# Unsplit first-layer factors, a PReLU of two operations, and products summed in a bank that is read between them

## The chip, the cores and the metric

The kernel runs on one core of one Trainium2 chip. The metric is the device time of one execution in microseconds (us). Five engines work side by side: PE (TensorE, matmuls), DVE (VectorE), ACT (ScalarE), POOL (GpSimd) and SP (SyncE, which issues the transfers). They wait for each other by semaphores. Matmuls write into eight accumulation banks (PSUM); the other engines read these.

## The reference, cut to what matters

```
attn = softmax(mask(q @ k.T / 8)) @ v          # 4 batches, 8 heads, 576 positions, 64 each
x = attn as [2304, 512]                        # 2304 tokens
h = max(x @ w1, x @ w2, x @ w3)                # first network, 512 -> 768
x = h @ moe_w_out                              # 768 -> 512
h = x @ w_in                                   # second network, 512 -> 2048
g = max(h, 0) + alpha * min(h, 0)              # PReLU, one slope for each hidden column
return g @ moe2_w_out                          # 2048 -> 512
```

## The kernel before, in words

Every matmul works on a number split in two: a high part, rounded to the short form that TensorE multiplies fast, and a low part, the rest. A product is the sum of three matmuls (high by high, high by low, low by high; `PAIRS`). A split costs a cast for the high part, mostly on ACT, and a subtraction for the low part, mostly on DVE.

**Stage 1** (0 to about 318 us) is laid out by a planner, `Weave`, from costs, positions and rings of buffers given with `add(...)`. It runs the attention and the first network for batches 0 to 2 and turns the weights, which come as 64-bit floats, into 32-bit words: `from_double` loads them, `rebase` (ACT) and `join_words` (DVE) make a word. `pair_tasks` (L506) forms the factors of the second network: 16 calls, eight for w_in and eight for w_out. For w_in each call makes four factors, splits them (`store_tasks`) and stores high and low part to DRAM tiles `wh` (list `hd`).

**Stage 2** (about 318 to 388 us) is `last_net` (L684): the first network of batch 3. After 12 ordinary gate units it goes through six groups k = 3 to 8 of seven Strassen-like products each. A product is six matmuls of 288 columns into a bank of its own; DVE adds each bank to sums that lie in SBUF (u, v, w), takes the greatest of three gates (`greatest`) and, after the third, splits it (`make_lows`). Beside this ACT and POOL prepare inputs x2 of the second network for the next block (`early_sums`, `early_split`): POOL makes four sums, ACT casts the high part, POOL subtracts the low part, SP stores both (`xd`). At the end come eight output products.

**Stage 3** (about 388 to 748 us) is the second network: 3 blocks of 768 tokens, each with 8 units n (24 in all). `h_products(n)` gives seven products of six matmuls with 384 columns into two banks `ph` in turn; `o_units(n-1)` gives 12 pieces of three matmuls with 256 columns into banks `po`. The loop at the end weaves the two by hand through `units_before`. The copy of the first product goes to ACT; DVE adds the others to sums in SBUF (L1191); `hidden` then makes the PReLU, in `slopes` (two ACT operations) and `join` (one on DVE), and `split_g` splits the result. `sums` forms what the next layer's Strassen form needs. `defer(s, step)` puts a step off by s products. `load_h` fetches the factors for unit n+2 during unit n, high and low part, up to 512 KB each.

At a block's end (n = 7, 15, 23) the first pieces of `kept_units` use the two `ph` banks directly after the unit's products, the first bank in six matmuls (two pieces), the second in three; `prepare` splits kept sums for them, twice in product 5 of that unit.

## Time and profile before

| what | value |
|---|---|
| times of three runs | 749.99, 750.4, 751.33 us (median 750.4) |
| profiled execution | span 747.7 us; its time lies outside the profile, the median of the runs is 2.7 us above the span |
| PE busy | 732.9 us (98%), 5560 matmuls |
| DVE busy | 640.3 us (86%) |
| ACT busy | 464.5 us (62%) |
| POOL busy | 28.7 us (4%) |
| TensorE's granted clock | 1.00 of full speed in every slice |

The span is the time from the first to the last instruction on the engines. "Busy" is the time in which an engine executes something; an average over the span says nothing of one stage, so the rows further down are taken by stage. The ends of matmuls are modelled: consecutive matmuls overlap in the records.

### The profile page before, as it was taken

How to read it: one execution, taken by the hardware profiler on the slowest of the kernel's cores; microseconds unless marked ns; L12 is line 12 of the kernel's file. 1: busy time of each engine (PE TensorE's matmuls, PEld its weight loads, DVE VectorE, ACT ScalarE, POOL GpSimd, SP SyncE). 2: the span in 40 equal slices, each digit the busy share in tenths (PEclk: the TensorE clock that was granted, in tenths of full speed). 3: DMA queues.
4: the chain of work that ended last, by engine and by line, in shares of the span. 5: the costliest groups of instructions: out<-in, count | busy, mean ns of one | idle time of the engine just before them, and what ended most of it. 6: DMA issues, size and time to landing. Idle time of an engine off the chain costs nothing.

```text
span 747.7 us, 16003 instructions
## 1 busy us (share of the span) xinstructions
PE 732.9 (98%) x5560; PEld 710.3 (95%) x5560; DVE 640.3 (86%) x1711; ACT 464.5 (62%) x1254; POOL 28.7 (4%) x42
## 2 busy tenths in 40 slices
PE   5899999999999999999999999999999999999998
PEld 4699999999999999999999999999999999999997
DVE  4899999899898999478868898888989888988896
ACT  5987889568684788423345666634666654556571
POOL 1000000000000000023500000000000000000000
PEclk9999999999999999999999999999999999999999
DMA  7477769996999765779899789999789999867362
GB/s 248 155 244 227 234 206 337 342 342 244 323 318 340 252 219 208 253 267 332 306 319 400 266 293 332 383 401 372 265 286 316 364 401 369 289 236 254 118 201 77
DMA packets 88929, 211.96 MB, mean 283 GB/s; under 512 B 11024, under 2 KB 41232, under 8 KB 88848
## 3 DMA queue, kind: packets, MB, share of 16 engines
q1 hardware_dynamic: 88848, 210.94, 80.4%
q8 instruction: 44, 0.72, 0.4%
q14 instruction: 37, 0.30, 0.1%
HBM read 154.80 MB, written 56.10 MB: 282 GB/s over the span
## 4 chain that ended last, share of the span: by engine, by line
PE 94%; ACT 2%; DMA 2%; DVE 1%; issue 0%; SPq 0%; ACTq 0%; DVEq 0%
PE bank L580 24%; PE ph L1185 23%; PE po L986 15%; PE bank L602 10%; PE bank L753 4%; PE po L992 4%; PE ph L986 3%; PE bank L317 3%; PE bank L392 2%; PE bank L367 2%; PE po L996 2%; ACT e L332 1%; DMA wh<-w 1%; DMA k<-in_kTs 0%; PE po L1185 0%; DMA wo<-w 0%
## 5 line engine op out<-in xcount | busy, mean ns | idle before, releaser
L1185 PE MATMUL ph<-x,w 128*128 128x384 f32 x990 | 200.1, 337 | 0.0
L580 PE MATMUL bank<-x,w 128*128 128x288 f32 x1440 | 197.5, 296 | 0.0
L580 PEld LDWEIGHTS bank<-x,w 128*128 128x128 f32 x1440 | 191.8, 188 | 2.1
L1185 PEld LDWEIGHTS ph<-x,w 128*128 128x128 f32 x990 | 166.3, 188 | 1.0
L986 PE MATMUL po<-w,g 128*128 128x256 f32 x936 | 135.6, 281 | 0.0
L986 PEld LDWEIGHTS po<-w,g 128*128 128x128 f32 x936 | 130.1, 189 | 0.4
L1191 DVE TENSOR_TENSOR c<-ph,c 128x384 f32<-128x384 f32 x165 | 89.5, 555 | 30.5 <-PE ph L1185 27.4
L979 ACT CAST g<-c 128x384 fp32r<-128x384 f32 x93 | 47.0, 505 | 91.1 <-DVE c L1169 51.7
L602 PE MATMUL bank<-h,w 128*128 128x288 f32 x576 | 79.4, 297 | 0.0
L602 PEld LDWEIGHTS bank<-h,w 128*128 128x128 f32 x576 | 76.9, 188 | 0.9
L256 ACT CAST w<-word 128x512 fp32r<-128x512 f32 x100 | 58.0, 590 | 24.8 <-DMA wh<-w 7.9
L332 ACT ACTIVATE e<-e,nm 96x128 f32<-96x128 f32 (+2 forms) x176 | 68.1, 396 | 6.1 <-DVE nm L325 5.9
L259 DVE TENSOR_TENSOR w<-word,w 128x512 fp32r<-128x512 f32 x100 | 63.4, 642 | 9.2 <-ACT w L256 8.9
L1129 ACT ACTIVATE c<-c 128x384 f32<-128x384 f32 x96 | 50.5, 526 | 32.9 <-DVE c L1191 31.8
L1130 ACT ACTIVATE c<-c,nalpha 128x384 f32<-128x384 f32 x96 | 59.2, 617 | 3.1
L1134 DVE SCALAR_TENSOR_TENSOR c<-c 128x384 f32<-128x384 f32 x96 | 53.1, 553 | 6.1 <-ACT c L1130 6.1
L980 DVE TENSOR_TENSOR g<-c,g 128x384 fp32r<-128x384 f32 x96 | 53.0, 552 | 0.9 <-ACT g L979 0.5
L451 ACT ACTIVATE word<-raw 128x512 f32<-128x512 f32 x56 | 37.6, 682 | 14.6 <-DMA raw<-in_w 10.8
L980 DVE TENSOR_TENSOR g<-k,g 128x384 fp32r<-128x384 f32 x72 | 37.2, 558 | 7.5 <-ACT g L979 7.5
L992 PE MATMUL po<-w,g 128*128 128x512 f32 x120 | 43.0, 397 | 0.0
L457 DVE SCALAR_TENSOR_TENSOR word<-raw,word 128x512 uint32<-128x512 uint32 x56 | 38.8, 692 | 1.9
L1169 DVE TENSOR_TENSOR k<-c 128x384 f32<-128x384 f32 x72 | 37.9, 551 | 0.0
(107 smaller groups left out, 939.1 us busy)
## 6 DMA issues: line engine op xcount, KB each, us to landing
w<-wh SPq DMA_DIRECT2D x72, 512.0 KB, 5.3
raw<-in_w SPq DMA_DIRECT2D x50, 512.0 KB, 5.1
w<-wo SPq DMA_DIRECT2D x48, 512.0 KB, 5.8
w<-wp SPq DMA_DIRECT2D x36, 512.0 KB, 6.4
wh<-w SPq DMA_DIRECT2D x24, 512.0 KB, 5.0
xd<-xst SPq DMA_DIRECT2D x28, 384.0 KB, 3.2
x<-xd SPq DMA_DIRECT2D x28, 384.0 KB, 8.2
ws<-w SPq DMA_DIRECT2D x12, 512.0 KB, 5.4
```

Source lines behind the costliest of these rows:

```text
L256: (nc.scalar.copy if e == "ACT" else nc.vector.tensor_copy)(out_, in_)
L259: nc.vector.tensor_tensor(out=out_, in0=x, in1=y, op=ALU.subtract)
L332: nc.scalar.activation(tl[ek][:nq, j, i, :nk], tl[ek][:nq, j, i, :nk], AF.Exp, bias=tl["nm", u][:nq, j, i:i + 1], scale=-1.0, accum_out=tl ...
L580: nc.tensor.matmul(acc, words["gate", f, g][:, wi, cc * P:(cc + 1) * P], xt[b, cc, hf][:, xi, :], start=n == 0, stop=n == 3 * NCC - 1)
L602: nc.tensor.matmul(acc, words["mix", f][:, wi, dc * P:(dc + 1) * P], st["h", hf, f][:, xi, :], start=n == 0, stop=n == 3 * NF1 - 1)
L980: return g, lambda: nc.vector.tensor_tensor(out=g[:, 1], in0=x, in1=g[:, 0].bitcast(F32), op=ALU.subtract)
L986: nc.tensor.matmul(bank[:, NH * half:NH * (half + 1)], g[:, gi, t * P:(t + 1) * P], w[:, wi, off:off + NH], start=first and i == 0, stop=l ...
L992: nc.tensor.matmul(bank.rearrange("p (s n) -> p s n", n=NH), g[:, 0, t * P:(t + 1) * P], w[:, :, off:off + NH], start=first, stop=last)
L1130: nc.scalar.activation(a, a, AF.Copy, scale=nalpha[:, f:f + 1])
L1134: nc.vector.scalar_tensor_tensor(out=a, in0=h, scalar=0.0, in1=a, op0=ALU.max, op1=ALU.add)
L1185: nc.tensor.matmul(bank, words["h", n, i][:, wi, off + c * P:off + (c + 1) * P], x2h[blk, k, c][:, xi, :], start=m == 0, stop=m == 5)
L1191: nc.vector.tensor_tensor(out=out_, in0=bank, in1=other, op=ALU.add)
```

## The change

Three parts, in the words of the code:

- **Factors split at each fetch.** `wh` holds the factors of w_in as plain 32-bit words. `keep_task` stores them as they are in place of `store_tasks`, so the 32 splits of stage 1 fall away. `load_h` fetches half the bytes. After each fetch `high_h` (ACT, a cast) and `low_h` (DVE, a subtraction) split the factor: four of each for every unit n, 96 of each in all; those of units 0 and 1 stand in `last_net`, those of unit n+1 in unit n at its products 0, 1, 4, 5 and 6.
- **PReLU in two operations.** `g = max(h, alpha * h)` if the slope is at most 1. For a greater slope the sign of h, of alpha and of the second layer's factor is turned: `flip_sb` holds the sign bits, `join_words` puts them into the 16 words of w_out, `sign_sb` is 1 or -1. `hidden` is then one ACT operation (copy times sign) and one on DVE (times alpha, then the greater of the two). alpha is loaded at the start of the program instead of after stage 1.
- **Products that add up in a bank.** In both networks the products 11, T2, T3 and T4 go into one bank `grown`, with `start=False` after the first. Between two of them ACT copies what stands there (u, v, w). Products 21, T1 and 22 use the other bank or banks of their own; in stage 3 the last product adds to T1. DVE does three additions from banks in place of seven for each unit or group. The order of the products, `units_before` and the product at which `load_h` runs are changed. Unit 0 keeps four banks.

```diff
-    hd = [[dram.tile([P, 2, DM], F32, name=f"wh{q}_{i}") for i in range(4)] for q in range(NQ)]
+    hd = [[dram.tile([P, DM], F32, name=f"wh{q}_{i}") for i in range(4)] for q in range(NQ)]
...
+            nc.vector.tensor_scalar(out=a, in0=a, scalar1=3, scalar2=flip_sb[:, flip:flip + 1],
+                                    op0=ALU.logical_shift_left, op1=ALU.bitwise_xor)
...
+    def keep_task(key, ak, n, place, pos, given):
+        add(load(n // 2), lambda _: nc.sync.dma_start(place[:, :n], tl[ak][:, :n].bitcast(F32)), pos,
+            needs=[given], gives=[("stored", key)], uses=[ak])
...
+            def follow(left=0):
+                while len(lows) > left:
+                    h, t = lows.pop(0)
+                    nc.vector.tensor_tensor(out=h[:, 1], in0=t, in1=h[:, 0].bitcast(F32), op=ALU.subtract)
+                for hf, f, t in highs:
+                    h = st["h", hf, f] = hp.tile([P, 2, HALF], F32R, tag="x", name="h")
                     nc.scalar.copy(h[:, 0], t)
                     lows.append((h, t))
+                highs.clear()
+
+            u, v, w = (new() for _ in range(3))
+            grown = bank()[:, :HALF]
+            product(grown, w0, 0, "11")
+            nc.scalar.copy(u, grown)
+            follow()
+            yield
+            x = bank()[:, :HALF]
+            product(x, w0, 256, "21")
             add(u, x, u)
+            follow()
+            keep(0, 0, u)
+            yield
+            product(grown, sb, 256, "T2", False)
+            nc.scalar.copy(v, grown)
+            follow()
+            yield
+            y = bank()[:, :HALF]
+            product(y, sa, 0, "T1")
+            add(v, y, v)
+            follow()
+            yield
+            product(grown, sb, 0, "T3", False)
+            nc.scalar.copy(w, grown)
+            add(w, y, w)
+            follow()
+            keep(1, 1, w)
+            yield
+            x = bank()[:, :HALF]
+            product(x, sa, 256, "22")
             add(v, x, v)
...
+            product(grown, w1_, 256, "T4", False)
...
-                nc.sync.dma_start(t[:, :, :m].bitcast(F32), hd[n % NQ][i][:, :, :m])
+                nc.sync.dma_start(t[:, 1, :m].bitcast(F32), hd[n % NQ][i][:, :m])
+    def high_h(n, i):
+            nc.scalar.copy(t[:, 0, :m], t[:, 1, :m].bitcast(F32))
+    def low_h(n, i):
+            nc.vector.tensor_tensor(out=t[:, 1, :m], in0=t[:, 1, :m].bitcast(F32),
+                                    in1=t[:, 0, :m].bitcast(F32), op=ALU.subtract)
...
+    for m, i, n in ((0, 0, -12), (0, 2, -11), (0, 1, -5), (0, 3, -4), (1, 0, 3), (1, 2, 4), (1, 1, 5), (1, 3, 6)):
+        splits.setdefault(gates + n, []).append(lambda m=m, i=i: high_h(m, i))
+        splits.setdefault(gates + n + 1, []).append(lambda m=m, i=i: low_h(m, i))
...
-            nc.scalar.activation(a, h, AF.Relu, scale=-1.0)
-            nc.scalar.activation(a, a, AF.Copy, scale=nalpha[:, f:f + 1])
-            defer(1, join)
+            nc.scalar.activation(a, h, AF.Copy, scale=sign_sb[:, f:f + 1])
+            defer(soon, join)
...
-            nc.vector.scalar_tensor_tensor(out=a, in0=h, scalar=0.0, in1=a, op0=ALU.max, op1=ALU.add)
+            nc.vector.scalar_tensor_tensor(out=a, in0=h, scalar=alpha_sb[:, f:f + 1], in1=a,
+                                           op0=ALU.mult, op1=ALU.max)
...
+        product(2, grown, start=False)
+        nc.scalar.copy(v, grown)
         due()
         yield
+        product(3, other)
+        due()
+        yield
+        product(4, grown, start=False)
+        nc.scalar.copy(w, grown)
+        load_h(n + 2, (0, 2))
+        add(w, other, w)
+        hidden(n, 1, 1, w)
+        due()
+        yield
+        product(5, grown, start=False)
...
+        hidden(n, 1, 0, grown, 0)
...
+        product(6, other, start=False)
         load_h(n + 2, (1, 3))
+        add(v, other, v)
...
-        units_before = [i * 12 // 7 for i in range(8)]
+        units_before = [0, 1, 2, 3, 4, 8, 10, 12]
...
+                for half, m in {0: (("high", 0),), 1: (("low", 0),), 4: (("high", 2), ("low", 2), ("high", 1)),
+                                5: (("low", 1), ("high", 3)), 6: (("low", 3),)}.get(i, ()):
+                    (high_h if half == "high" else low_h)(n + 1, m)
```

How the change moves instructions is shown at three places. In the rows a name is a tile with its number, `<-` goes from what is written to what is read, and the waits name the engine or the transfer queue that the instruction waits for.

First ACT in stage 2, from the end of group 5 into group 6. `h` is a hidden tile's high part, `xst` an early split of x2, `t<-bank` a copy from a bank. Before:

```order
L766 CAST h_5557<-t_5364 128x288 [waits DVE_49]
L766 CAST h_5572<-t_5343 128x288 [waits DVE_49]
L211 CAST xst_5575<-xs_5459 128x384 [waits DMAHW6_49,DMAHW0_49,Pool_49]
L771 COPY t_5585<-bank_5578 128x288 [waits PE_49,Activation_49]
L211 CAST xst_5598<-t_5539 128x384 [waits DMAHW3_49,Pool_49]
L211 CAST xst_5619<-xs_5460 128x384 [waits DMAHW4_49,DMAHW0_49]
L211 CAST xst_5641<-t_5540 128x384 [waits DMAHW5_49]
L771 COPY t_5664<-bank_5657 128x288 [waits PE_49]
```

and in the changed kernel:

```order
L211 CAST xst_5458<-xs_5353 128x384 [waits DMAHW6_49,DMAHW0_49,Pool_49]
L786 COPY t_5461<-bank_5464 128x288 [waits PE_49,Activation_49]
L779 CAST h_5473<-t_5295 128x288 [waits DVE_49]
L211 CAST xst_5485<-xs_5354 128x384 [waits DMAHW3_49,DMAHW0_49,Pool_49]
L796 COPY t_5462<-bank_5464 128x288 [waits PE_49,Activation_49]
L211 CAST xst_5504<-t_5426 128x384 [waits DMAHW4_49,Pool_49]
L805 COPY t_5463<-bank_5464 128x288 [waits DVE_49,PE_49]
L211 CAST xst_5524<-xs_5353 128x384 [waits DMAHW5_49]
L821 COPY t_5537<-bank_5464 128x288 [waits DVE_49,PE_49]
```

One copy in a group has become three or four, each from the bank into which the next product of the group is added, and they stand between the casts of x2, which wait for POOL and for transfers.

Second PE in one unit of the second network (`ph` are the two banks, `po` the banks of the woven pieces). Before:

```order
L1185 MATMUL ph_7891<-x30_7175,w_7625 128x384 [waits DVE_49]
L1185 MATMUL ph_7891<-x30_7175,w_7625 128x384 x2
L1185 MATMUL ph_7891<-x31_7177,w_7625 128x384 x3
L986 MATMUL po_7798<-w_7511,g_7854 128x256 x3
L1185 MATMUL ph_7892<-x40_7197,w_7709 128x384 [waits DMAHW3_49,DVE_49]
L1185 MATMUL ph_7892<-x40_7197,w_7709 128x384 x2
L1185 MATMUL ph_7892<-x41_7199,w_7709 128x384 x3
L986 MATMUL po_7836<-w_7558,g_7878 128x256 [waits DMAHW1_49]
L986 MATMUL po_7836<-w_7558,g_7878 128x256 x5
L1185 MATMUL ph_7891<-x50_7226,w_7709 128x384 [waits DVE_49]
L1185 MATMUL ph_7891<-x50_7226,w_7709 128x384 x2
```

and in the changed kernel:

```order
L1240 MATMUL ph_7933<-x30_7060,w_7769 128x384 [waits DVE_49]
L1240 MATMUL ph_7933<-x30_7060,w_7769 128x384 x2
L1240 MATMUL ph_7933<-x31_7062,w_7769 128x384 x3
L1040 MATMUL po_7692<-w_7488,g_7894 128x256 x3
L1240 MATMUL ph_7932<-x40_7081,w_7716 128x384 [waits Activation_49]
L1240 MATMUL ph_7932<-x40_7081,w_7716 128x384 x2
L1240 MATMUL ph_7932<-x41_7083,w_7716 128x384 x3
L1040 MATMUL po_7724<-w_7488,g_7894 128x256 x6
L1040 MATMUL po_7733<-w_7533,g_7897 128x256 [waits DMAHW6_49]
L1040 MATMUL po_7733<-w_7533,g_7897 128x256 x5
L1240 MATMUL ph_7932<-x50_7122,w_7769 128x384 [waits Activation_49]
L1240 MATMUL ph_7932<-x50_7122,w_7769 128x384 x2
```

Before, products alternate between two banks and wait for DVE. Now four of them go into one bank (`ph_7932` here) and wait there for ACT, which copies it between them; a longer stretch of woven pieces stands ahead of the sixth product.

Third DVE around products 4 to 6 of a block's last unit. Here `g<-k` is the low part of a kept sum (`prepare`), `c<-ph` reads a bank, and `w<-w` the low part of a fetched factor. Before:

```order
L1191 TENSOR_TENSOR c_7190<-ph_7092,c_7169 128x384 [waits DVE_49,PE_49]
L1191 TENSOR_TENSOR c_7117<-ph_7092,c_7117 128x384
L980 TENSOR_TENSOR g_7173<-c_7144,g_7173 128x384 [waits Activation_49]
L980 TENSOR_TENSOR g_7213<-k_6236,g_7213 128x384 [waits Activation_49]
L980 TENSOR_TENSOR g_7216<-k_6384,g_7216 128x384 [waits Activation_49]
L1191 TENSOR_TENSOR c_7169<-ph_7091,c_7169 128x384 [waits DVE_49,PE_49]
L1134 SCALAR_TENSOR_TENSOR c_7192<-c_7190,c_7192 128x384
L1191 TENSOR_TENSOR c_7117<-ph_7092,c_7117 128x384 [waits DVE_49,PE_49]
```

and in the changed kernel:

```order
L1246 TENSOR_TENSOR c_6990<-ph_6987,c_6990 128x384 [waits Activation_49]
L909 TENSOR_TENSOR w_6917<-w_6917 128x512 [waits DMAHW5_49,Activation_49]
L1034 TENSOR_TENSOR g_7108<-k_6128,g_7108 128x384 [waits Activation_49]
L1034 TENSOR_TENSOR g_7111<-k_6277,g_7111 128x384 [waits Activation_49]
L1187 SCALAR_TENSOR_TENSOR c_7079<-c_6990,alpha_sb_65,c_7079 128x384 [waits DVE_49]
L1187 SCALAR_TENSOR_TENSOR c_7114<-ph_6986,alpha_sb_65,c_7114 128x384 [waits Activation_49]
L909 TENSOR_TENSOR w_6967<-w_6967 128x512 [waits DMAHW7_49]
L1246 TENSOR_TENSOR c_6989<-ph_6987,c_6989 128x384 [waits PE_49]
```

Both readings that free the `ph` banks for the first kept pieces (`c_7114<-ph_6986` and `c_6989<-ph_6987`) now stand behind the low parts of two kept sums and of fetched factors.

## Rows read from the trace of the kernel before

**Rows 1.** The page's head and its first part: busy time of each engine.

```profile
span 747.7 us, 16003 instructions
PE 732.9 (98%) x5560; PEld 710.3 (95%) x5560; DVE 640.3 (86%) x1711; ACT 464.5 (62%) x1254; POOL 28.7 (4%) x42
```

**Rows 2.** Windows: stretch, length, busy (count) of PE PEld DVE ACT POOL, PEclk, DMA share, GB/s.

```profile
0.00:40.00 40.00, 28.85 (x275) 22.69 (x276) 27.85 (x170) 32.48 (x140) 3.51 (x17) 1.00 0.63 204
40.00:740.00 700.00, 699.74 (x5253) 683.58 (x5252) 609.66 (x1536) 432.06 (x1115) 25.22 (x25) 1.00 0.83 290
```

**Rows 3.** Timeline of PE, 288-column matmuls of stages 1 and 2: start, us, what.

```profile
316.24 19.20 PE L580 MATMUL bank<-x,w 128*128 128x288 f32 x144
335.28 33.76 PE L753 MATMUL bank<-x,w 128*128 128x288 f32 x252
```

**Rows 4.** Timeline of PE and DVE: last product of one unit, first two of the next, its last.

```profile
440.00 1.22 PE L1185 MATMUL ph<-x,w 128*128 128x384 f32 x6
...
441.25 0.56 DVE L1191 TENSOR_TENSOR c<-ph,c 128x384 f32<-128x384 f32 x1 [0.74 <-PE ph L1185]
...
441.75 1.21 PE L1185 MATMUL ph<-x,w 128*128 128x384 f32 x6
...
443.15 1.22 PE L1185 MATMUL ph<-x,w 128*128 128x384 f32 x6
...
451.58 0.69 PE L1185 MATMUL ph<-x,w 128*128 128x384 f32 x3
```

**Rows 5.** ACT's groups by form: count | busy, mean ns of one | idle before, releaser.

```profile
L979 ACT CAST g<-c 128x384 fp32r<-128x384 f32 x93 | 47.0, 505 | 91.1 <-DVE c L1169 51.7 <-DVE c L1134 33.9 <-PE po L986 5.4
...
L256 ACT CAST w<-word 128x512 fp32r<-128x512 f32 x84 | 51.5, 624 | 17.6 <-DMA wp<-w 5.3 <-DMA wh<-w 5.0 <-DVE word L457 2.9
...
L1130 ACT ACTIVATE c<-c,nalpha 128x384 f32<-128x384 f32 x96 | 59.2, 617 | 3.1
...
L1195 ACT COPY c<-ph 128x384 f32<-128x384 f32 x24 | 11.3, 470 | 11.7 <-PE ph L1185 11.7
...
L771 ACT COPY t<-bank 128x288 f32<-128x288 f32 x6 | 2.4, 393 | 5.1 <-PE bank L753 5.1
```

**Rows 6.** DVE's groups by form.

```profile
L1191 DVE TENSOR_TENSOR c<-ph,c 128x384 f32<-128x384 f32 x165 | 89.5, 555 | 30.5 <-PE ph L1185 27.4 <-ACT c L1195 2.4
L259 DVE TENSOR_TENSOR w<-word,w 128x512 fp32r<-128x512 f32 x84 | 56.8, 685 | 6.3 <-ACT w L256 6.2
...
L733 DVE TENSOR_TENSOR t<-bank,t 128x288 f32<-128x288 f32 x42 | 18.4, 453 | 4.2 <-PE bank L753 1.5 <-ACT xst L211 1.1 <-ACT t L771 0.8
```

**Rows 7.** Timeline at the end of the first block (unit 7): the readings of the banks, and PE.

```profile
475.63 0.55 DVE L1191 TENSOR_TENSOR c<-ph,c 128x384 f32<-128x384 f32 x1
...
476.22 0.53 ACT L1129 ACTIVATE c<-c 128x384 f32<-128x384 f32 x1 [1.15 <-DVE c L1191]
...
476.50 1.77 PE L986 MATMUL ph<-w,g 128*128 128x256 f32 x13
476.56 0.56 DVE L1191 TENSOR_TENSOR c<-ph,c 128x384 f32<-128x384 f32 x1
```

**Rows 8.** Timeline of ACT in stage 2, the first group and group 6.

```profile
336.06 0.43 ACT L211 CAST h<-t 128x288 fp32r<-128x288 f32 x1 [0.75 <-DVE t L591]
336.40 0.76 ACT L211 CAST x<-t 128x288 fp32r<-128x288 f32 x2
337.07 0.39 ACT L771 COPY t<-bank 128x288 f32<-128x288 f32 x1
...
357.72 0.52 ACT L211 CAST xst<-t 128x384 fp32r<-128x384 f32 x1 [2.38 <-POOL t L831]
...
362.45 0.51 ACT L211 CAST xst<-xs 128x384 fp32r<-128x384 f32 x1 [3.10 <-DMA xd<-xst]
```

**Rows 9.** Timeline of POOL: the third sum of x2 in group 6, from which ACT casts.

```profile
356.57 1.11 POOL L831 TENSOR_TENSOR t<-xs 128x384 f32<-128x384 f32 x1
```

**Rows 10.** DMA issues: count, KB each, median us from issue to landing.

```profile
w<-wh SPq DMA_DIRECT2D x72, 512.0 KB, 5.3
```

More of the change, by code (lines that the diff above doesn't have):

```diff
@@ L445, in from_double @@
             uses=[rk])
-        add((("DVE", 1050),), lambda _: join_words(tl[rk], tl[ak]), pos, needs=[("up", key)],
+        add((("DVE", 1050),), lambda _: join_words(tl[rk], tl[ak], flip), pos,
+            needs=[("up", key)] + ([("slopes",)] if flip is not None else []),
             gives=[ak], uses=[rk, ak])
@@ L528, in pair_tasks @@
         if layer == 0:
-            store_tasks(("h", q, 0), ek, DM, [(0, hd[q][0][:, :, :])], pos, ek)
-            parts_ = ((1, ok, DM, [(0, hd[q][1][:, :, :])]), (2, sk[0], DM, [(0, hd[q][2][:, :, :])]),
-                      (3, sk[1], half, [(0, hd[q][3][:, :, :half])]))
+            keep_task(("h", q, 0), ek, DM, hd[q][0], pos, ek)
+            for i, k, n in ((1, ok, DM), (2, sk[0], DM), (3, sk[1], half)):
+                keep_task(("h", q, i), k, n, hd[q][i], late, ("sums", s))
+            return
         else:
@@ L746, in last_net, with product @@
             new = kept_temp if g == 0 else temp
-            def product(w, off, name):
-                bank_ = bank()[:, :HALF]
+            def product(bank_, w, off, name, start=True):
                 m = 0
@@ L753, in product, with keep @@
                         nc.tensor.matmul(bank_, w[:, wi, off + c * P:off + (c + 1) * P],
-                                         factors[name, c][:, xi, :], start=m == 0, stop=m == 5)
+                                         factors[name, c][:, xi, :], start=start and m == 0,
+                                         stop=m == 5, skip_group_check=True)
                         m += 1
-                return bank_
-            def greatest(hf, j, c):
+            def keep(hf, j, c):
                 if g == 0:
@@ L766, in greatest @@
                     nc.scalar.copy(h[:, 0], t)
                     lows.append((h, t))
-            x = product(w0, 0, "11")
-            u = new()
-            nc.scalar.copy(u, x)
-            yield
-            x = product(sb, 256, "T2")
-            v = new()
-            add(v, x, u)
-            make_lows()
+                highs.clear()
[3 more added lines that the diff above has]
+            nc.scalar.copy(u, grown)
@@ L793, in last_net @@
-            add(w, x, w)
+            x = bank()[:, :HALF]
+            product(x, sa, 256, "22")
             add(v, x, v)
-            make_lows()
-            greatest(1, 1, w)
+            follow()
+            keep(1, 0, v)
             yield
-            x = product(sa, 256, "22")
+            product(grown, w1_, 256, "T4", False)
             load_factors(k + 4)
-            add(v, x, v)
-            greatest(1, 0, v)
-            make_lows(1)
+            follow()
+            if g == 0:
+                last = new()
+                nc.scalar.copy(last, grown)
+                keep(0, 1, last)
+            else:
+                keep(0, 1, grown)
@@ L886, in load_ow, with slope_tasks, slopes @@
             nc.sync.dma_start(t.bitcast(F32), (od1 if which == "o1" else od2)[a][i])
+    def slope_tasks(pos):
+        def slopes(_):
+            nc.vector.tensor_scalar(out=flip_sb, in0=alpha_sb, scalar1=1.0, scalar2=None, op0=ALU.is_gt)
+            nc.vector.tensor_scalar(out=flip_sb, in0=flip_sb, scalar1=31, scalar2=None,
+                                    op0=ALU.logical_shift_left)
+        add(load(2), lambda _: nc.sync.dma_start(alpha_sb, alpha), pos, gives=[("alpha",)])
+        add((("DVE", 400),), slopes, pos + 2, needs=[("alpha",)], gives=[("slopes",)])
     homes = [("gate", f, g) for f in range(NF1) for g in range(3)] + [("mix", f) for f in range(NF1)]
@@ L935, in attention_maxout_prelu_kernel @@
             load_ow()
+        for step in splits.pop(n, ()):
+            step()
         if n - 1 in ready:
@@ L968, in attention_maxout_prelu_kernel @@
     NH = DM // 2
[L969 to L970 removed]
+    sign_sb = osp.tile([P, NF2], F32, name="sign")
+    nc.vector.tensor_scalar(out=sign_sb, in0=alpha_sb, scalar1=1.0, scalar2=-2.0, op0=ALU.is_gt, op1=ALU.mult)
+    nc.vector.tensor_scalar(out=sign_sb, in0=sign_sb, scalar1=1.0, scalar2=None, op0=ALU.add)
+    nc.vector.tensor_tensor(out=alpha_sb, in0=alpha_sb, in1=sign_sb, op=ALU.mult)
     gts, kept, accs, res = {}, {}, {}, {}
@@ L1173, in h_products, with product @@
         blk = n // NQ
-        banks = [ps_h.tile([P, DM], F32, tag="ph", name="ph")[:, :HB] for _ in range(2)]
-        if n == 0:
-            banks += [ps_o.tile([P, DM], F32, tag="po", name="po")[:, :HB] for _ in range(2)]
-        def product(k):
-            bank = banks[(1, 0, 3, 2)[k % 4] % len(banks)]
+        def product(k, bank, start=True):
             slot[0] += 1
```

132 lines of the change are left out of this document (72 added, 60 removed).

## The prediction, as it was put on record

> **What bounds the kernel now.** I read the busy times first, then windows, then timelines. PE is busy 732.9 of 747.7 us [rows 1]. The windows say where the rest lies: 11.15 us of it before 40 us, and from 40 to 740 us PE works 699.74 of 700 us at a granted clock of 1.00 [rows 2], that is at the 2.4 GHz level. Nothing that PE waits for is left there, though DVE is busy 609.66 us of the same stretch. The matmuls of before and after are the same in number and form, so relief for DVE, ACT or the transfers gains nothing there, and every new wait of PE is paid in full. The pace comes from timelines: 288-column matmuls follow each other by 0.132 us ((335.28-316.24)/144) and 0.133 us, a product's end lies 0.16 us behind the start of what follows (19.20-19.04) [rows 3]. In the second network a unit lasts 11.58 us (451.58-440.00); six matmuls of 384 columns and three of 256 take 1.40 us, with three more 1.75 us, so a product counts 1.05 and a piece 0.35 us; a product's result can be read 1.25 us after its start (441.25) [rows 4]. What I look for is therefore each place where a bank comes free later than PE needs it.
>
> **Start and stage 1.** The load of alpha and two small DVE operations now stand ahead of the first transposes' supply, where PE is idle 11.15 us [rows 2]: I add +0.2. The 32 splits that fall away there cost ACT 0.62 and DVE 0.69 us each [rows 5, 6], 20 and 22 us in all, beside PE that is never short after 40 us: worth nothing, except that the planner's changed order switches five times fewer between kinds of matmul: -0.3. Sum -0.1.
>
> **Transfers.** 72 fetches of 512 KB and 24 smaller ones are halved. They land in 5.3 us [rows 10] and PE waited for none of them: gain 0. Two of a unit's four are now fetched 6 us (from 5.60 to 11.58, below) ahead of the first split; a landing 2 us later than the median still leaves ACT free for its next copy, so no loss either. The new split of unit 1's factors in stage 2 can come before its tile has landed, since two of them are fetched only some 5 us before: 0 to 0.7, I take +0.3.
>
> **Hand-offs in stage 2.** Products of one group now meet in one bank. The third may start after ACT has copied the first: result 0.80+0.16+0.03, copy 0.39 [rows 5], and 0.05 for the way to PE (an estimate by the 0.03 to 0.04 that the others show), together 1.43 us; PE needs it after two products, 1.60 us. The spare is 0.17 us, and only if ACT is idle. It is not in four of the 18 hand-offs:
> - First group: the cast of h at 336.06 and two casts stand ahead of the copy, which ended at 337.46 [rows 8], 2.18 us after the group's start at 335.28 [rows 3]. Before, DVE read that copy later; now PE does: 2.23 less 1.60, +0.65.
> - Between the third and fourth group three casts of h and one of x2 (0.51) come first: +0.5.
> - Group 6: the copy ahead of T4 stands behind the cast of T2, which waits for POOL's third sum, ended at 357.68 [rows 9], cast at 357.72 [rows 8]. Ended at 358.24, plus 0.39 and 0.05, is 358.7, where PE would be due at 358.1 (335.28 + 27 products of 0.80 + the 1.15 above): +0.6 if POOL keeps its time, +1.6 if it is a microsecond later, since its own loads are issued by the same program steps. I take +1.5.
> - Group 7: a copy stands behind the cast that waited 3.10 us for a store [rows 8]: 0 to 1.5, I take +0.6.
>
> Together +3.3, with ends 1.0 and 5.5.
>
> **Units of the second network.** With 1, 1, 1, 1, 4, 2, 2 pieces after its products they start at 0, 1.40, 2.80, 4.20, 5.60, 8.05 and 9.80 us. ACT's copy takes 0.47 [rows 5], so a hand-off is free 1.25+0.47+0.05 = 1.77 us after its product's start. The third and fifth product then have 1.03 us to spare, the sixth (8.05 against 7.37) 0.7. The next unit's first product needs the bank that PReLU now reads directly on DVE: result at 9.30, behind two factor casts on ACT to 9.6, copy with sign 0.62 [rows 5], two operations of 0.56 on DVE [rows 6]: about 10.8 against 11.58, 0.8 to spare. Work on DVE hardly changes: four additions fewer of 0.56 are 2.2 us, four low parts more (three of 0.69, one smaller) 2.4. On ACT four casts (2.3) come, two copies (0.9) come, and four activations (2.5) go. In about nine units (3 to 6, 10 to 14) two casts and two low parts for the next block also stand in the way, 0.5 each; the spare of 0.7 shrinks to 0.2 and may be gone in some: +0.1 each, +1.0, with ends 0 and 3.
>
> **Ends of blocks.** At unit 7 DVE read the banks at 475.63 and 476.56; its second reading ended at 477.12, and PE, which began on the banks at 476.50, needs the second one six matmuls later, at 477.2 [rows 7]. There was next to nothing to spare. Now both readings stand behind two kept sums and the split of two factors: on ACT sign copy to 8.6 us of the unit, two factor casts at 0.52 pace to 9.6, two casts to 10.45, sign copy to 11.07; on DVE the join ends at 12.0 and the last addition at 13.1. PE wants the banks at 11.58 and, delayed, 12.8: +0.8. So also at unit 15; unit 23 has no factors to split. +1.6, with ends 0.8 and 2.6.
>
> **Sum.** -0.1 + 0.3 + 3.3 + 1.0 + 1.6 = +6.1 us on the profiled execution, 747.7 to 753.8. The median of the runs, 750.4, lies 2.7 above the span; I keep that: 756.5.
>
> **Rivals.**
> (a) *The hand-offs hide.* POOL and the store of x2 have their loads earlier, the boundary's casts find ACT free, and what remains is 0 to +1.5, about 751. For it: four of the five terms rest on an order of waits that I timed by hand within half a microsecond.
> (b) *The lag repeats.* If the next unit's first product waits for the join in every unit, 0.3 us in 20 units is +6 more: 762.5. It starts when DVE's queue runs 0.8 us late. For it: DVE's load of about 87% in this stage does not fall. Against it: the sequence repeats each 11.58 us, and I find the spare positive. The Trainium skill ("Perfetto Trace Analysis", Optimizing Tensor Performance, Matmuls) wants matmul groups to rotate through different banks, so that one is emptied while the next works; this change gives that up for four of seven products, and by that rule the result would be (b).
> (c) *Faster, by PE's pace.* The rows give 0.132 us for 288 columns and 0.175 for 384 (1.05/6): both 0.46 ns for a column, where one clock of the 2.4 GHz level is 0.417 ns. If readers of the banks hold PE back, and fewer DVE readings release it, the place is every one of 5560 matmuls; the whole gap of 9% is 60 us, a tenth is 6 us, and it decides from 1% of the pace on, 7 us, where it eats my sum. A fifth of the gap gives 750.4-12+6 = 744. Against it: the pace is 0.132 and 0.133 in two stretches with other neighbours [rows 3], and readings of banks only pass from DVE to ACT: eight per unit before and eight after. The Trainium skill ("Perfetto Trace Analysis", Identifying the Most-Contended Engine) says that matmul busy share does not show how near PE is to its limit, and that the share of weight loads does better; that is 710.3 us or 95% here [rows 1], which leaves little to (c) as well.
> (d) *Faster, by stage 1.* The planner's new order fills part of the 11.15 us at the start: -3, 747.5. Against it: the splits that vanish come later than 40 us.
>
> **How the numbers follow.** A measurement of this kernel can tell about 0.2%, 1.5 us, from no change: 748.9 to 751.9. Forecast (slower by 3 to 9 us) 0.59; (a) 0.20, all within 0.2%; (b) 0.12; (c) 0.06; (d) 0.03. Slower 0.71, same 0.20, faster 0.09. The low ends of my terms sum to +1.7 (-0.1 + 0 + 1.0 + 0 + 0.8), the high ends to +11.7 (-0.1 + 0.7 + 5.5 + 3.0 + 2.6); the range from 750 to 763.5 takes in these, (b) and most of (a), and leaves out about 0.2.
>
> **What would show it.** Right: PE idle ahead of the 288-column products' first matmul, released by ACT, some 0.6 to 1.5 us each, in groups 3, 6 and 7; idle ahead of matmuls into `ph` at units 7 and 15, released by DVE, 0.3 to 0.5 us each; small ones in units 3 to 6 and 10 to 14; all other paces as before. Wrong: PE still at 99.9% from 40 to 740 us (then (a)); the same idle in every unit (b); a pace below 0.130 us for 288 columns (c); less idle before 40 us (d).

## The result, and the profile after

The changed kernel takes 758.74 us (median of 4 runs, 757.81 to 759.96); the kernel before, on the same chip, 750.87 us (749.99 to 753.37). The ratio is 1.0102, 95% interval 1.0081 to 1.0124: slower by 1.0%, 7.9 us, where 6.1 us was forecast, inside the range. The profiled execution of the changed kernel is one of its slower two (759.65); its span, 757.9, lies 10.2 above that of before. In that run time and span differ by 1.75 us. If they do so in before as well, its profiled execution took about 749.5, some 0.9 to 1.4 under the medians shown of it.

The head and first part of the page after, against [rows 1], and the windows against [rows 2]:

```profile
span 757.9 us, 15861 instructions
...
PE 737.5 (97%) x5560; PEld 711.5 (94%) x5560; DVE 629.6 (83%) x1670; ACT 466.6 (62%) x1269; POOL 28.4 (4%) x42
```

```profile
0.00:40.00 40.00, 28.85 (x270) 22.38 (x271) 27.23 (x164) 31.74 (x138) 3.53 (x17) 1.00 0.61 202
40.00:740.00 700.00, 694.21 (x5188) 675.62 (x5188) 591.76 (x1482) 432.24 (x1128) 24.86 (x25) 1.00 0.73 248
```

DVE has 11 us less to do, ACT 2 us more, the start is as it was, and PE, which worked 699.74 of the 700 us from 40 to 740, now works 694.21, at the same granted clock. The windows understate the loss: a product's last matmul is drawn 0.16 us into what follows, so a stall of x shows as an idle of about x - 0.16. The sums below therefore go by the starts of products in PE's timeline; the end of the 42 products alone is taken as drawn, 0.16 us late in both kernels:

| part | before | after | difference |
|---|---|---|---|
| span's start to the first product of group 3 | 335.28 | 334.53 | -0.75 |
| 42 products of the six groups | 33.76 | 37.62 | +3.9 |
| output products of stage 2 | 18.92 | 19.84 | +0.9 |
| second network, of it: | 356.3 | 362.5 | +6.2 |
| - units 1 to 6 and 9 to 14 | | | +4.35 |
| - units 7 and 15 with their block ends | | | +2.2 |
| - units 0, 8, 16 to 23 | | | -0.4 |

PE's timeline of the changed kernel in stage 2 (start, us, what, and idle before with its releaser) shows where the groups broke:

```profile
334.53 1.75 PE L759 MATMUL bank<-x,w 128*128 128x288 f32 x12
336.67 17.11 PE L759 MATMUL bank<-x,w 128*128 128x288 f32 x126 [0.39 <-ACT t L786]
354.07 3.46 PE L759 MATMUL bank<-x,w 128*128 128x288 f32 x24 [0.30 <-ACT t L786]
358.82 4.23 PE L759 MATMUL bank<-x,w 128*128 128x288 f32 x30 [1.29 <-ACT t L805]
363.26 7.57 PE L759 MATMUL bank<-x,w 128*128 128x288 f32 x54 [0.21 <-ACT t L796]
371.09 1.06 PE L759 MATMUL bank<-x,w 128*128 128x288 f32 x6 [0.26 <-ACT t L805]
371.98 2.18 PE L614 MATMUL bank<-h,w 128*128 128x288 f32 x15
374.47 1.82 PE L614 MATMUL bank<-h,w 128*128 128x288 f32 x9 [0.31 <-ACT h L779]
```

All five breaks among the products are released by ACT's copy from the shared bank (L786 is u, L796 v, L805 w). From start to start they cost 0.64 (group 3), 0.58 (group 6), 1.54 (group 6, last product), 0.46 (group 7) and 0.5 (group 8); the sixth is ahead of an output product. A delay of 0.15 ahead of group 7's last product is too short to be drawn. The other 12 of the 18 hand-offs pass without a wait.

The longest of them, in the timeline of all engines:

```profile
356.92 1.00 POOL L854 TENSOR_TENSOR t<-xs 128x384 f32<-128x384 f32 x1
357.96 0.51 ACT L211 CAST xst<-t 128x384 fp32r<-128x384 f32 x1 [2.33 <-POOL t L854]
...
358.38 0.39 ACT L805 COPY t<-bank 128x288 f32<-128x288 f32 x1
...
358.82 0.66 PE L759 MATMUL bank<-x,w 128*128 128x288 f32 x3 [1.29 <-ACT t L805]
```

POOL's third sum ends at 357.92, the cast of it at 358.47, only then ACT turns to the bank, and PE goes on at 358.82; it had been due 1.4 us earlier.

Unit 4 of the second network (434.98 to 447.60), one of those with preparation of x2 beside it and the one that lost most (1.05 us), from ahead of ACT's third copy to the next unit:

```profile
441.88 0.93 ACT L1033 CAST g<-c 128x384 fp32r<-128x384 f32 x2 [1.67 <-DVE c L1187]
...
442.71 0.51 ACT L1353 CAST xst<-t 128x384 fp32r<-128x384 f32 x1
...
443.13 0.47 ACT L1310 COPY c<-ph 128x384 f32<-128x384 f32 x1
443.64 0.55 DVE L1246 TENSOR_TENSOR c<-ph,c 128x384 f32<-128x384 f32 x1
443.65 1.31 PE L1240 MATMUL ph<-x,w 128*128 128x384 f32 x6 [0.25 <-ACT c L1310]
444.23 0.62 ACT L1183 ACTIVATE c<-c,sign 128x384 f32<-128x384 f32 x1 [0.63 <-DVE c L1246]
444.75 0.49 ACT L1353 CAST xst<-xs 128x384 fp32r<-128x384 f32 x1
...
445.15 1.14 ACT L903 CAST w<-w 128x512 fp32r<-128x512 f32 x2
...
445.80 0.69 DVE L909 TENSOR_TENSOR w<-w 128x512 fp32r<-128x512 f32 x1 [1.61 <-ACT w L903]
446.19 0.57 ACT L1183 ACTIVATE c<-ph,sign 128x384 f32<-128x384 f32 x1
446.41 0.61 DVE L1187 SCALAR_TENSOR_TENSOR c<-c,alpha_sb 128x384 f32<-128x384 f32 x1
...
446.94 0.61 DVE L1187 SCALAR_TENSOR_TENSOR c<-ph,alpha_sb,c 128x384 f32<-128x384 f32 x1
...
447.60 0.62 PE L1240 MATMUL ph<-x,w 128*128 128x384 f32 x2 [0.17 <-DVE c L1187]
```

And the same place in unit 18, without preparation:

```profile
663.20 1.13 ACT L903 CAST w<-w 128x512 fp32r<-128x512 f32 x2
663.84 0.69 DVE L909 TENSOR_TENSOR w<-w 128x512 fp32r<-128x512 f32 x1 [1.19 <-ACT w L903]
...
664.23 0.57 ACT L1183 ACTIVATE c<-ph,sign 128x384 f32<-128x384 f32 x1
...
664.98 0.61 DVE L1187 SCALAR_TENSOR_TENSOR c<-ph,alpha_sb,c 128x384 f32<-128x384 f32 x1
...
666.31 1.04 PE L1240 MATMUL ph<-x,w 128*128 128x384 f32 x5
```

In unit 18 the join that frees the bank ends at 665.59, 0.72 before PE needs it. In unit 4 ACT waits 1.67 us for DVE ahead of the casts of g (0.97 at the same place of unit 18), and then a cast of x2 stands ahead of the copy of w (443.13): PE's sixth product comes 0.41 late. Another cast of x2 stands ahead of the factors' casts (445.15); the sign copy from the bank starts at 446.19 though the product could be read from about 444.9; DVE waits 1.61 us for the factor's cast (1.19 in unit 18), with both joins behind that wait, and the next unit's first product comes 0.33 late. Units 3, 5 and 11 to 13 lose 0.3 at this second place, and PE's matmuls follow each other about 0.1 later behind a break.

The end of the first block, against [rows 7]:

```profile
481.91 1.03 DVE L1034 TENSOR_TENSOR g<-k,g 128x384 fp32r<-128x384 f32 x2 [0.24 <-ACT g L1033]
482.20 0.57 ACT L1183 ACTIVATE c<-ph,sign 128x384 f32<-128x384 f32 x1
...
482.86 0.61 DVE L1187 SCALAR_TENSOR_TENSOR c<-c,alpha_sb 128x384 f32<-128x384 f32 x1
483.39 0.61 DVE L1187 SCALAR_TENSOR_TENSOR c<-ph,alpha_sb,c 128x384 f32<-128x384 f32 x1
...
484.05 0.98 PE L1040 MATMUL ph<-w,g 128*128 128x256 f32 x6 [0.69 <-DVE c L1187]
```

PE wanted the banks at 483.2 and got the first at 484.05, 12.4 us after the unit's start at 471.61. The second bank, six matmuls later, came another 0.25 late.

The halved fetches land sooner than [rows 10], 3.3 against 5.3 us, and ACT is never idle ahead of one of the 96 casts that read them:

```profile
w<-wh SPq DMA_DIRECT2D x72, 256.0 KB, 3.3
```

### The profile page after: what moved, and what is told of

It reads as the page before. It is cut to its first block, busy times and chain, and to the rows that moved or that the text cites. A ratio compares the mean times of both kernels' runs of the same rounds, so it can differ in the third digit from the quotient of the medians.

```text
span 757.9 us, 15861 instructions
## 1 busy us (share of the span) xinstructions
PE 737.5 (97%) x5560; PEld 711.5 (94%) x5560; DVE 629.6 (83%) x1670; ACT 466.6 (62%) x1269; POOL 28.4 (4%) x42
## 4 chain that ended last, share of the span: by engine, by line
PE 68%; DVE 17%; ACT 5%; DMA 4%; issue 3%; POOL 1%; SPq 0%; POOLq 0%; ACTq 0%; DVEq 0%
PE bank L592 26%; PE bank L614 10%; PE ph L1240 9%; PE po L1040 7%; DVE w L909 3%; PE ph L1040 3%; DVE g L1034 3%; DVE c L1187 3%; PE bank L318 3%; PE po L1046 3%; PE bank L393 3%; PE bank L368 2%; DVE c L1246 2%; DVE k L1228 2%; ACT w L903 1%
## 5 line engine op out<-in xcount | busy, mean ns | idle before, releaser
L909 DVE TENSOR_TENSOR w<-w 128x512 fp32r<-128x512 f32 x96 | 60.3, 629 | 31.3 <-ACT w L903 26.8
L1183 ACT ACTIVATE c<-c,sign 128x384 f32<-128x384 f32 x73 | 45.0, 617 | 57.9 <-DVE c L1246 57.8
L903 ACT CAST w<-w 128x512 fp32r<-128x512 f32 x96 | 51.8, 562 | 0.0
L1034 DVE TENSOR_TENSOR g<-c,g 128x384 fp32r<-128x384 f32 x96 | 49.2, 550 | 0.9 <-POOL g L1033 0.6
L257 ACT CAST w<-word 128x512 fp32r<-128x512 f32 x68 | 39.4, 602 | 14.1 <-DVE word L535 7.1
L1246 DVE TENSOR_TENSOR c<-ph,c 128x384 f32<-128x384 f32 x73 | 40.1, 552 | 7.7 <-PE ph L1240 6.8
L260 DVE TENSOR_TENSOR w<-word,w 128x512 fp32r<-128x512 f32 x68 | 43.6, 651 | 2.8 <-ACT w L257 2.8
L1187 DVE SCALAR_TENSOR_TENSOR c<-c,alpha_sb 128x384 f32<-128x384 f32 x73 | 44.7, 612 | 0.3 <-ACT c L1183 0.2
```

What stands on the lines that cost most here:

```text
L903: nc.scalar.copy(t[:, 0, :m], t[:, 1, :m].bitcast(F32))
L909: nc.vector.tensor_tensor(out=t[:, 1, :m], in0=t[:, 1, :m].bitcast(F32), in1=t[:, 0, :m].bitcast(F32), op=ALU.subtract)
L1034: return g, lambda: nc.vector.tensor_tensor(out=g[:, 1], in0=x, in1=g[:, 0].bitcast(F32), op=ALU.subtract)
L1187: nc.vector.scalar_tensor_tensor(out=a, in0=h, scalar=alpha_sb[:, f:f + 1], in1=a, op0=ALU.mult, op1=ALU.max)
L1246: nc.vector.tensor_tensor(out=out_, in0=bank, in1=other, op=ALU.add)
```

## The experiments

The theory: PE loses time where the ACT or DVE operation that frees a shared bank stands in its queue behind other work, above all the casts and low parts of the fetched factors and the casts of x2. The rivals: the hand-off inside one bank is too long by itself; or DVE and ACT are simply full. Lengths of units and groups are again from PE's timeline, and every ratio is to the kernel before on the same chip.

### Factors split once

```diff
-            keep_task(("h", q, 0), ek, DM, hd[q][0], pos, ek)
...
+            store_tasks(("h", q, 0), ek, DM, [(0, hd[q][0][:, :, :])], pos, ek)
...
-                nc.sync.dma_start(t[:, 1, :m].bitcast(F32), hd[n % NQ][i][:, :m])
+                nc.sync.dma_start(t[:, :, :m].bitcast(F32), hd[n % NQ][i][:, :, :m])
```

> Edit: the changed kernel, but the factors of w_in are split once in stage 1 and stored split, as before; no high_h and low_h. Theory (PE waits for banks whose readers on ACT and DVE stand behind the fetched factors' casts and low parts): the second network, 362.5 us in the changed kernel against 356.3 before, loses the waits of units 3 to 6 and 11 to 14 (4.3 us) and most of those at the two block ends (2.2 us, 0 to 0.4 left), so 356.0 to 357.0; the third wait in the last group of stage 2 (0.4) goes too; stage 1 gets back its 0.9 us. Span 757.9 down to about 752. Rival (products that meet in one bank are too slow to hand over, whatever stands beside them): units 3 to 6 and 11 to 14 keep 0.3 us or more each, the second network stays at 359 or more, the span at 755 or more.

Measured: span 750.1, ratio to before 1.0017 (1.0002 to 1.0032). Units 2 to 6 and 10 to 14 are 11.59 us, all of them; the block ends lie 0.2 under before; the second network takes 355.2 us, 7.3 less than in the changed kernel and 1.1 less than before. The wait in group 8 is gone. In stage 2 the waits of groups 3, 6 and 7 stay (0.93, 0.58, 0.69, 0.47). So the same shared bank costs nothing in the second network once the splits are away, and all its loss there hangs on them. The first rival falls for the second network. In stage 1 nothing came back that can be told from its spread: over all runs with the changed kernel's stage 1 unaltered, the first product of group 3 comes 329.0 to 332.2 us after PE's first matmul (330.7 before).

### last_net in banks of its own

```diff
-            product(grown, sb, 256, "T2", False)
-            nc.scalar.copy(v, grown)
...
+            x = product(sb, 256, "T2")
+            v = new()
+            add(v, x, u)
...
```

> Edit: the changed kernel with the seven products of last_net in banks of their own and summed on DVE in the old order; the rest as changed. Theory (ACT's copies of the shared bank come late in stage 2): the 42 products take 33.8 us as before (37.6 in the changed kernel) and the output products lose most of their 0.9, so the span falls by 4.0 to 4.8, to 753.1 to 753.9. Rival (the casts of the fetched factors in stage 2 hold ACT and DVE up by themselves): the 42 products stay above 35 us.

Measured: the 42 products take 33.8 us, as expected, and yet the span is 757.7 and the ratio 1.0121 (1.0093 to 1.0149): nothing was won. The output products grew from 19.84 to 23.75 us. The timeline of this run, PE and then DVE and ACT, and its windows there (us, PE busy, granted clock, DMA share, GB/s):

```profile
368.03 2.84 PE L614 MATMUL bank<-h,w 128*128 128x288 f32 x15
372.42 0.40 PE L614 MATMUL bank<-h,w 128*128 128x288 f32 x1 [1.54 <-ACT h L778]
373.39 6.83 PE L614 MATMUL bank<-h,w 128*128 128x288 f32 x38 [0.57 <-DVE h L752]
```

```profile
370.35 0.69 DVE L898 TENSOR_TENSOR w<-w 128x512 fp32r<-128x512 f32 x1
...
371.93 0.43 ACT L778 CAST h<-t 128x288 fp32r<-128x288 f32 x1 [1.31 <-DVE t L745]
```

```profile
372.00:374.00 2.00, 1.01 (x5) 1.00 1.06 349
374.00:376.00 2.00, 2.00 (x11) 0.54 1.06 384
376.00:377.00 1.00, 1.00 (x6) 0.50 0.97 375
```

The products no longer wait, so PE comes 3.9 us earlier to the output products, and the hidden tiles that these need are not ready: on DVE, busy nearly all of this time, their maxima stand between the low parts (L898) of the next stage's factors. After those gaps the granted clock fell to 0.50 for 3.4 us (matmuls of 288 columns 0.24 apart instead of 0.13), which added about 1.5 us. The expectation held in its first half and failed in its second: the waits had covered a later one.

### Splits at later places

```diff
-                for half, m in {0: (("high", 0),), 1: (("low", 0),), 4: (("high", 2), ("low", 2), ("high", 1)),
-                                5: (("low", 1), ("high", 3)), 6: (("low", 3),)}.get(i, ()):
-                    (high_h if half == "high" else low_h)(n + 1, m)
+                for half, m, d in {0: (("high", 0, 1), ("low", 1, 0)), 1: (("low", 0, 1), ("high", 3, 0)),
+                                   2: (("low", 3, 0),), 5: (("high", 2, 1),),
+                                   6: (("low", 2, 1), ("high", 1, 1))}.get(i, ()):
+                    if n > 1 or d:
+                        (high_h if half == "high" else low_h)(n + d, m)
```

> Edit: the changed kernel with the same casts and low parts of fetched factors at other places: none between product 4 and the reader of product 5's bank (tile 2's cast after that reader, tile 1's after product 6, their low parts and tile 3 from there into the next unit). The work of each engine is the same. Theory (their place in the queue ahead of the reader costs, not their amount): units 3 to 6 and 11 to 14 fall from 4.3 us over before to under 1.5 together, the two block ends from 1.1 each to 0.4 or less, the second network from 362.5 to 357 to 358.5. Rival (DVE and ACT are full in these units): it moves by less than 1.5 us.

Measured: span 752.3, ratio 1.0054 (1.0033 to 1.0075). The second network takes 358.3 us. Both block ends fall to +0.07. Units 11 to 14 keep 0.16 to 0.19 each, units 5 and 6 0.2, but units 3 and 4 still 0.75 and 0.63, so the units together kept 2.4, not under 1.5. With the same work on each engine two thirds of the second network's loss were their places alone; what holds units 3 and 4 is left open.

### The PReLU of two operations alone, on the kernel before

```diff
-            nc.scalar.activation(a, h, AF.Relu, scale=-1.0)
-            nc.scalar.activation(a, a, AF.Copy, scale=nalpha[:, f:f + 1])
+            nc.scalar.activation(a, h, AF.Copy, scale=sign_sb[:, f:f + 1])
...
```

> Edit: the kernel before with the PReLU of two operations alone (slopes loaded early, sign bits put into the words of w_out). Theory (ACT and DVE are covered by PE there): nothing, the span 747.7 within 0.7 us; the start 0.2 later. Rival (ACT's 96 operations fewer matter): the span under 746.5.

Measured: span 747.7, as expected, ratio 0.998 (0.996 to 0.9999). Units 7, 9, 15, 17 and 23 are each 0.2 us shorter than before: small waits at the block ends, which the profile of before hid under its overlaps. Unit 0 was 1.3 longer: its first copy stood behind an output copy that waited 1.95 us for a store. Unit 1 was 0.2 longer. So this part gains up to 1 us, and no more is to be had where PE is busy throughout.

### Of the change, the PReLU and the second network's bank sums

This is the last_net of before and the factors split once, that is the first two edits together.

> Edit: the changed kernel with the factors split once in stage 1 and last_net in banks of its own; so of the change only the PReLU of two operations and the sums in a bank in the second network stay. The 3.9 us that the output products lost when last_net alone was put back are, by the theory, the fetched factors' casts and low parts in the queues ahead of the last hidden tiles; they are gone here. Expected: 42 products 33.8 us, output products 18.9 to 19.0, second network 355.2 (as with the factors split once), span 746.0 to 747.2, that is 0.5 to 1.5 under before. Rival (the loss in the output products comes from the sums' order or from the loads of alpha, not from the splits): output products stay above 20 us, span above 748.

Measured: span 748.4, median 749.68 against 751.09, ratio 0.9981 (0.9968 to 0.9994): the one version with an interval under 1 that holds bank sums, faster by 0.2%. The 42 products take 33.76, the output products 19.1 us: the 3.9 us lost there had been the splits'. The span is over the 746.0 to 747.2 expected, because the second network is 357.0, not 355.2: unit 0 again 1.2 longer, behind a copy that waits for a store, and unit 16 0.5, once. The gains in units 7, 9, 15, 17 and 23 are those of the PReLU alone, to 0.01 us; the bank sums add nothing to them.

### Casts of x2 two products later

```diff
-    ready = {X_SPLIT + 22 * half + 2 * k: (1, half, k) for half in range(2) for k in range(7)}
+    ready = {X_SPLIT + 24 * half + 2 * k: (1, half, k) for half in range(2) for k in range(7)}
```

> Edit: the changed kernel with the seven early splits of x2 in groups 6 to 8 of last_net two steps (two products) later, so that ACT's copies of the shared bank in groups 6 and 7 stand ahead of the casts that wait for POOL and for the stores. Theory: the wait ahead of the last product of group 6 (1.54 us) falls to 0.2 or less and the one in group 7 (0.45) to 0.2 or less; the 42 products take 35.6 to 36.2 us (37.6 in the changed kernel); span down by 1.0 to 2.0. Rival (the copy itself, 0.40 us, and its way are too long for two products): both waits stay.

Measured: span 758.1, ratio 1.0099 (1.0082 to 1.0117), no gain. The waits it aimed at fell to 0.0 and 0.0, and that of group 6's third product from 0.58 to 0.2, but the last product of group 7 now waits 1.23 and the third of group 8 1.44; the 42 products take 37.2 us. The third product of group 8 after the move, and what stood ahead of its copy:

```profile
367.02 0.51 ACT L211 CAST xst<-xs 128x384 fp32r<-128x384 f32 x1 [2.60 <-DMA xd<-xst]
...
367.44 0.39 ACT L786 COPY t<-bank 128x288 f32<-128x288 f32 x1
...
367.88 1.32 PE L759 MATMUL bank<-x,w 128*128 128x288 f32 x8 [1.18 <-ACT t L786]
```

The cast waited 2.60 us for the store that frees its buffer. The places were right, the remedy was not: at its new place too a cast of x2 that waits holds the next copy.

### Sums on DVE, splits kept

```diff
-        product(2, grown, start=False)
-        nc.scalar.copy(v, grown)
...
+        bank = product(2)
+        add(u, bank, u)
         hidden(n, 0, 0, u)
...
-        units_before = [0, 1, 2, 3, 4, 8, 10, 12]
+        units_before = [i * 12 // 7 for i in range(8)]
```

> Edit: the changed kernel with the second network's products in alternating banks, summed on DVE, and pieces woven as before; factors still split at each fetch, PReLU of two operations. Theory on place alone: readers of banks no longer pass through ACT, but the factors' low parts still stand in DVE's queue, and DVE gets four additions of 0.56 us more in a unit: about 369 us of DVE work for a second network of 356, so it becomes the bound in the units with preparations: +0.5 to 1.5 each in units 3 to 6 and 10 to 14, the span 756 to 766. Rival (the shared bank is what costs): the waits vanish and the second network takes 357 us or less.

Measured: span 777.9, ratio 1.0385 (1.0369 to 1.0402); the second network takes 380.9 us. Units with preparation grow by 1.2 to 2.0, plain ones (18 to 22) by 0.2, block ends by 2.6 and 2.7; DVE is busy 19.2 of 20 us in the first kind and 19.3 in the second (before 17.5 and 16.6):

```profile
440.00:460.00 20.00, 18.28 (x116) 17.40 (x116) 19.20 (x41) 9.67 (x21) 0.00 (x0) 1.00 0.61 205
680.00:700.00 20.00, 20.00 (x134) 19.70 (x133) 19.32 (x40) 12.35 (x26) 0.00 (x0) 1.00 0.58 183
```

So the three parts belong together: the bank sums free the DVE time that the splits at each fetch take. The direction was as expected; the loss was larger than I gave, in the units, at the block ends and in units 9 and 17 (1.8 each). In stage 2 of this run, whose code there is that of the changed kernel, one hand-off in group 6 cost 3.0 us with POOL late, and the granted clock was 0.50 for 3.4 us behind it.

### Extra work in units without a wait

```diff
+            if n in (17, 18) and i in (2, 4) or n in (20, 21) and i in (1, 6):
...
+                if n < 20:
+                    nc.scalar.copy(extra[0][:, 0], src)
+                else:
+                    nc.vector.tensor_tensor(out=extra[1][:, 0], in0=src, in1=src, op=ALU.subtract)
```

> Edit: the changed kernel with extra work in units that show no wait: in units 17 and 18 one more ACT cast of 384 columns after product 2 and one after product 4, in units 20 and 21 one more DVE subtraction of 384 columns after product 1 and one after product 6 (the places and sizes that the preparation of x2 has in units 3 to 6 and 11 to 14); their results are not used. Theory (the order on ACT, casts ahead of the readers of banks, makes the waits of 0.5 to 0.6 a unit): units 17 and 18 grow by 0.3 to 0.6 each, units 20 and 21 by less than 0.2. Rival (DVE's amount of work makes them): units 20 and 21 grow, 17 and 18 do not.

Measured (a single run, span 760.5): units 17 and 18 grow by 0.17 and 0.10, units 20 and 21 not at all. Neither theory had it: the order on ACT alone costs little, DVE's amount alone nothing. A new theory follows: the two late together.

### Both kinds together

```diff
+            if n in (17, 18, 20, 21) and i in (1, 2, 4, 6):
...
+                if i in (2, 4) and n < 20:
+                    nc.scalar.copy(extra[0][:, 0], src)
+                if i in (1, 6):
+                    for _ in range(1 if n < 20 else 2):
+                        nc.vector.tensor_tensor(out=extra[1][:, 0], in0=src, in1=src, op=ALU.subtract)
```

> Edit: as in the run with extra work in waitless units, but in units 17 and 18 both kinds at once (two ACT casts and two DVE subtractions each, as the preparation of x2 has them), and in units 20 and 21 four DVE subtractions each and no cast. Alone, the two casts cost 0.17 and 0.10 us a unit, the two subtractions nothing. New theory (the spare of a unit is eaten only when ACT and DVE are both late, since the factor's cast waits for ACT, its low part for the cast, and PReLU's join stands behind that low part): units 17 and 18 grow by 0.4 to 0.6 each, like units 11 to 13, units 20 and 21 by less than 0.3. Rival (the waits of units 11 to 13 come from something else in them, the transfers or the real data dependences): units 17 and 18 grow by 0.2 or less.

Measured (a single run, span 760.6): units 17 and 18 are 12.23 and 12.17 us against 11.59, +0.64 and +0.58 (units 11 to 13 of the changed kernel: 12.07 to 12.16). The two casts and two subtractions are enough to make the wait. Units 20 to 22 with four subtractions grow by 0.28, 1.35 and 0.30: DVE alone can do it too, with twice the amount, which I had put at under 0.3.

### Copies on DVE in last_net

```diff
-            nc.scalar.copy(u, grown)
+            nc.vector.tensor_copy(out=u, in_=grown)
```

(likewise v, w and the last copy), on top of the splits at later places.

> Edit: the version with the fetched factors split at later places (span 752.3), and in last_net the copies from the shared bank made by DVE instead of ACT. Theory (the waits of stage 2 come from what stands ahead of the copies on ACT: casts that wait for POOL, stores and the last gate's maximum): the waits in groups 3 and 6 (0.65, 0.58, 1.2 to 1.5) fall to 0.2 or less each; small ones of 0.1 to 0.3 may come in groups where DVE has maxima to take; the 42 products take 33.8 to 35.5 us (37.3 there), the span 748.5 to 751. Rival (two products are too short a time for any reader of the shared bank): the waits stay above 0.4 each and the products above 36 us.

Measured: span 755.4, ratio 1.0089 (1.0072 to 1.0106); the 42 products take 39.7 us, 2.4 more than with ACT's copies. The last product of group 6 no longer waits, but the third products of groups 3 and 6 wait longer, and that of group 8 waits 0.8:

```profile
336.78 17.43 PE L759 MATMUL bank<-x,w 128*128 128x288 f32 x126 [1.02 <-DVE t L786]
356.26 1.85 PE L759 MATMUL bank<-x,w 128*128 128x288 f32 x12 [2.04 <-DVE t L786]
```

And DVE ahead of the second of them, with POOL's sum beside it:

```profile
353.51 0.79 DVE L745 TENSOR_TENSOR t<-t 128x288 f32<-128x288 f32 x1
354.06 1.09 POOL L854 TENSOR_TENSOR t<-xs 128x384 f32<-128x384 f32 x1
354.22 1.25 DVE L776 TENSOR_TENSOR h<-t,h 128x288 fp32r<-128x288 f32 x1
...
355.76 0.45 DVE L786 COPY t<-bank 128x288 f32<-128x288 f32 x1
```

At a group's start DVE is behind with maxima and low parts, and beside POOL's sums they run slower: this low part took 1.25 us, where the same operation took 0.45 in the changed kernel. The expectation failed. What ACT's queue holds ahead of the copies makes the waits of groups 6, 7 and 8, as the runs with casts moved or taken away show (for group 3 it is read from the timeline alone), but DVE's queue is no better: in these groups neither engine is free within the two products, 1.60 us, that a shared bank leaves. The time alone is not too short, since groups 4 and 5 of the changed kernel have the same 1.60 us, copies on ACT and no wait.

## Why the prediction was right, and where not

**What bounds the kernel** held: with PE busy 99.96% from 40 us on, relief for DVE, ACT and transfers gained nothing; the PReLU alone, 96 ACT operations fewer, shows what there was to gain, 0.2 us at five places.

**Start and stage 1** (-0.1): -0.75 in the profile, inside the spread of 3 us that the same code shows there between runs, so neither shown nor refuted. The -0.3 in it was priced from no row; the traces show five changes between kinds of matmul fewer (118 against 123) and a 288-column matmul followed by another kind 0.22 us later instead of 0.13, together some 0.4 by estimate. **Transfers** (0): right. **Unit 1** (+0.3): +0.1 in that unit, but ACT never waited for a fetch, so the reason given for it is not shown.

**Hand-offs in stage 2** (+3.3): +3.9, and term by term 0.65 against 0.64, 0.5 against 0.58, 1.5 against 1.54, 0.6 against 0.46. What I missed were 0.5 in group 8, behind the casts of unit 0's factors (gone when the factors are split once), and 0.9 in the output products. These are nearly all of the 1.5 us by which stage 2 was under-priced.

**Units of the second network** (+1.0, with ends 0 and 3): +4.4 in units 3 to 6 and 10 to 14, outside these ends. This is the step that failed: "+0.1 each" for a spare that "shrinks to 0.2". The spare of a plain unit was right, 0.72 measured against 0.8. But of the four extra operations, 0.5 each, I took 0.5 in all off the spare. They add up along one chain: a cast of x2 delays the factor's cast, DVE waits for that cast (1.61 us idle in unit 4), and the joins queue behind it; DVE's own lateness delays the next casts on ACT (1.67 us idle there). The runs with extra work show it: 0.1 to 0.2 from ACT's two, 0 from DVE's two, 0.6 from all four. Four on DVE alone cost 0.3 and 1.35, so the spare can be used up by one engine too. Unit 10, which has sums of x2 on DVE but no casts, lost nothing.

**Ends of blocks** (+1.6): +2.2, the mechanism as told; PE got the first bank at 12.4 us of the unit where I had 12.1. Before had its own 0.2 there, which the PReLU removed, so the wait itself is 1.3 a block, where I had 0.8.

**One bank for four products.** With the factors split once, a shared bank costs nothing where 2.8 us lie between the starts of two of its products, and 0.5 to 0.9 a time in stage 2, where 1.6 do and casts of x2 or h stand in ACT's queue. The Trainium skill's rule that independent matmul groups should rotate through banks, so that one is emptied while the next works ("Perfetto Trace Analysis", Optimizing Tensor Performance, Matmuls), taken here for the products of one sum, is borne out by the second and not by the first.

The rivals: the hand-offs did not hide (a); the lag did not repeat in every unit (b), units 9, 10 and 17 to 22 are 11.59; the pace stayed at 0.133 and 0.174 (c); nothing of the start was filled (d). The sum came 1.8 short of the medians' difference, and 4.1 short of that of the two profiled executions, 2.3 of which is how those two stand to their medians. The hand-offs, the units and the block ends were all forecast too low; the total fell inside the range because the range was wide, not because the units' term was right.

## What to carry to other kernels

Where one engine never idles, as PE here, work taken from the others was worth next to nothing and every new wait cost in full: ask of each reader of a bank what stands ahead of it in its queue, and what that waits for in turn. A spare is used up along the chain across engines as well as on one engine, so add the extra operations of both before comparing with it. And when a wait is removed, look at what it had covered: in the run with last_net's own banks the output products lost all that the groups had won.

## What the runs showed of the hardware that was not expected

After gaps of PE of 1.54 and 0.57 us close together (in other runs after one of 2.85 and after 0.48 and 1.08) the granted clock stood at 0.50, the 1.2 GHz level, for 3.4 us each time, and 288-column matmuls came 0.24 us apart. A gap of 1.29 us in the changed kernel did not do this, nor one of 2.04 us in the run with copies on DVE. A DVE operation of the PReLU (multiply by a scalar for each partition, then maximum) took 0.61 us for 384 columns where an addition takes 0.55. Operations of DVE that read two tiles in SBUF took up to 2.8 times as long beside POOL's (1.25 against 0.45 us for 288 columns), though not all of them; those that read a bank kept their 0.45.
